# Attention with relative bias and a squared-ReLU feed-forward layer: products of 128 rows split into two row tiles of TensorE, the lower half behind the upper

## The chip, the cores and the metric

The kernel runs on one core of one Trainium2 chip. The metric is the device time of one execution in microseconds. PE is TensorE, DVE VectorE, ACT ScalarE, POOL GpSimd, SP SyncE; SP computes nothing here, its queue issues DMAs.

## The reference

Eight batches of eight heads, 576 positions, head size 64; then a feed-forward layer over the 4608 rows of 512.

```python
scores = 1.0 / np.sqrt(D) * np.matmul(q, k.transpose(0, 1, 3, 2))
scores = scores + bias_table[bucket].transpose(2, 0, 1)[None]     # bucket depends on |i - j| alone
scores = scores - np.max(scores, axis=-1, keepdims=True)
attn = np.exp(scores)
attn = attn / (np.sum(attn, axis=-1, keepdims=True) + 1e-09)
x = np.matmul(attn, v).transpose(0, 2, 1, 3).reshape(B * S, H * D)
h = np.maximum(x @ w_in, 0.0)                                     # 512 -> 2048
out = h * h @ w_out                                               # 2048 -> 512
```

Inputs and output are float32; the kernel works in float16 with float32 sums.

## The kernel before

**Attention.** A pair is two heads of one batch (32 pairs). Their q and k are turned so that head 0 lies on partitions 0 to 63 and head 1 on 64 to 127: on PE for the first two batches (L947), by DMA_TRANSPOSE issued on SP from the third on (L930). Scores come transposed, keys on partitions: for each block of 128 keys one matmul per head with 64 contracted rows and up to 512 queries (L815), one head on the upper 64 rows of PE's array, one on the lower 64, side by side. The last 64 queries go in eight matmuls of 64 columns (L822); the last 64 keys of both heads share one block, `kz`, that has zeros elsewhere, and use all 128 rows (L1012, L879). ACT takes exponentials out of PSUM into `pt` and `pm`, and DVE multiplies the diagonal bands by the bias's exponentials. The product with V (`values`) contracts 128 keys: for each tile of 128 queries one matmul of 130 columns with `pm` (L754) and eight of 65 with `pt` (L761); the 65th column gives the sum for the division. DVE divides into `x`, which is turned into `xt` by PE (L1078, first two batches) or by DMA_TRANSPOSE on SP (L795).

**Feed-forward.** Nine groups of 512 rows. The first layer has plain units of 128 x 512 (L1501, L1451) and units of seven products instead of eight (`by_sevens`, L1378). The second layer (`second`, L1204) also has seven products instead of eight, as 14 atoms of eight matmuls of 256 columns, all 128 rows. DVE and ACT read the sums out; SP issues the stores (L1260) and the loads of V from the third batch on (L368), POOL casts V.

**Order.** Nothing is issued as the loops run. Each step is an `Op` with costs by engine, dependences and buffers; `Plan.schedule` lays all of them out engine by engine, the earliest possible first and, among those, the least due time. `DUES` is a long table of due times that replaces those of some operations. The program is written in the order of the planned starts, and each engine works through its own part in that order. PE's mode in the plan is "r" for scores (64 rows) and "f" for the rest; a change of mode is charged with `SWITCH`. PSUM has two pairs of banks for scores (`sets_ps`, ring `r_set`) and four single banks (`g_ps`, ring `r_g`).

Of the kernel before, what the change touches and what calls it, by code (L numbers as in the profile page):

```python
# [30 lines left out]
DT_QK = 2  # L31
PERIOD, LEAD, FAST, FASTN = 8500, 2000.0, 3300.0, 6
# [93 lines left out]
class Ring:  # L126


    def __init__(self, n, in_order=False):
        self.free = [(0.0, i) for i in range(n)]  # L130
        self.in_order, self.made, self.taken = in_order, 0, 0


class Buf:


    def __init__(self, ring):
        self.ring, self.left, self.slot, self.until = ring, 0, None, 0.0
        self.turn, ring.made = ring.made, ring.made + 1


class Op:
    __slots__ = (
        "engs", "fn", "deps", "bufs", "due", "after", "mode",
        "users", "wait", "ready", "eng", "start", "end", "seq", "spare", "packets",
    )

    def __init__(self, engs, fn, deps, bufs, due, after, mode):
        self.engs, self.fn, self.bufs, self.due = engs, fn, bufs, due
        self.after, self.mode = after, mode  # L150
        self.deps = [d for d in deps if d is not None]
        self.users, self.ready, self.spare = [], after, 0.0
        self.start = self.end = self.eng = None
# [6 lines left out]
AGAIN = {"ACT": 30.0, "DVE": 30.0}  # L160

# [9 lines left out]
STAY = 0.0  # L171


class Plan:
# [3 lines left out]
    def add(self, engs, fn, deps=(), bufs=(), due=0.0, after=0.0, mode=None):  # L178
        op = Op(engs, fn, deps, list(bufs), due, after, mode)
        op.seq = len(self.ops)  # L180
        self.ops.append(op)
        for b in op.bufs:
            b.left += 1
        return op
# [6 lines left out]
    def schedule(self):  # L191
# [4 lines left out]
        for op in self.ops:  # L196
            op.wait = len(op.deps)
            for d in op.deps:
                d.users.append(op)
            if not op.wait:  # L200
                for e in op.engs:
                    waiting[e].append(op)
# [67 lines left out]
def act(n):  # L270
    return 174.0 + n / 1.2
# [1337 lines left out]
```

## Time and profile before

| | before |
|---|---|
| device time, two runs | 358.85 and 359.93 us, median 359.39 |
| profiled execution | span 358.7 us from first to last instruction, 0.7 us under the median |
| PE matmuls | x4290 |
| granted TensorE clock | 1.000 |
| PE, DVE, ACT, POOL busy | 97%, 83%, 76%, 48% |
| DMA | 44.37 MB, mean 124 GB/s |

The span is that of one execution; a run's time also holds what lies around it. A matmul's row lasts from its start until its results are out, so rows of neighbouring matmuls overlap, and PE counts as busy for as long as any of them runs.

### The profile page before, as it was taken

The numbers are of one execution on the slowest core, as the hardware profiler recorded it, in microseconds if no ns is written. First come the engines' busy times: TensorE is split into PE (matmuls) and PEld (weight loads), VectorE is DVE, ScalarE is ACT, GpSimd is POOL, SyncE is SP. The second block draws the span as 40 slices with busy tenths as digits, with TensorE's granted clock in tenths as the row PEclk, the third lists the DMA queues.
The fourth block names the chain that finished last, engine by engine and source line by source line (L and its number), as shares of the span: only waits on it lengthen the run. The fifth ranks groups of instructions, "written<-read, shape, count | busy, mean of one in ns | idle before, by whom it ended". The sixth has DMA issues, their size and how long they took to land.

```text
span 358.7 us, 10742 instructions
## 1 busy us (share of the span) xinstructions
PE 346.4 (97%) x4290; PEld 262.0 (73%) x4290; DVE 297.5 (83%) x673; ACT 272.6 (76%) x435; POOL 170.6 (48%) x289
## 2 busy tenths in 40 slices
PE   3988999999999999999999999999999999999996
PEld 3666788775587558877788568755867887888885
DVE  4888999666996799768896899798988798899993
ACT  4898997589966988678976887689889833899830
POOL 8886679698995896158478456221000000000000
PEclk9999999999999999999999999999999999999999
DMA  9999999999999999799999999863410032010023
GB/s 172 151 147 198 193 150 154 190 156 192 175 130 165 223 158 112 119 163 198 84 134 164 186 126 133 150 121 72 61 44 15 18 97 68 27 63 33 23 66 117
DMA packets 162210, 44.37 MB, mean 124 GB/s; under 512 B 145520, under 2 KB 162160, under 8 KB 162160
## 3 DMA queue, kind: packets, MB, share of 16 engines
q0 software_dynamic: 74208, 14.53, 54.6%
q1 hardware_dynamic: 87696, 28.86, 44.3%
q8 instruction: 33, 0.54, 0.6%
q10 hardware_dynamic: 256, 0.30, 0.3%
q14 instruction: 17, 0.14, 0.1%
HBM read 36.94 MB, written 9.44 MB: 129 GB/s over the span
## 4 chain that ended last, share of the span: by engine, by line
PE 88%; DMA 7%; POOL 2%; ACT 1%; issue 1%; DVE 0%; POOLq 0%
PE f L1204 31%; PE f L1501 20%; PE f L761 10%; PE st L815 8%; PE f L1378 7%; DMA w_in_sb<-in_moe_w_in_dram 5%; PE f L1451 3%; PE st L1378 3%; PE f L754 3%; PE st L1012 2%; DMA ks<-in_k_dram 2%; POOL va L368 2%; PE f L822 1%; PE f L1078 1%; POOL ks L368 0%
## 5 line engine op out<-in xcount | busy, mean ns | idle before, releaser
L997 ACT ACTIVATE pt<-st 128x1024 f16<-128x1024 f32 x112 | 111.1, 1031 | 23.0 <-PE st L815 22.8
L1501 PE MATMUL f<-xt,w_in_sb 128*128 128x512 f16 (+4 forms) x416 | 77.2, 330 | 0.0
L728 DVE TENSOR_TENSOR pt<-pt,tb_sb 128x512 f16<-128x512 f16 (+3 forms) x108 | 61.9, 581 | 12.6 <-ACT pt L997 9.3
L368 POOL DMA_DIRECT2D ks<-in_k_dram x79 | 55.9, 719 | 15.1 <-DMA kt<-ks 10.4
L1204 PEld LDWEIGHTS <-g 128*128 128x128 f16 x576 | 55.1, 98 | 7.6 <-issue 0.8
L368 POOL DMA_DIRECT2D qs<-in_q_dram x79 | 55.5, 712 | 8.1 <-DMA qt<-qs 6.2
L1530 ACT ACTIVATE rt<-f 128x512 f16<-128x512 f32 x80 | 47.3, 608 | 14.1 <-PE f L1501 12.7
L1501 PEld LDWEIGHTS <-w_in_sb 128*128 128x128 f16 x416 | 37.1, 98 | 26.7 <-issue 2.5
L761 PE MATMUL f<-va,pt 128*128 128x65 f16 x1280 | 53.2, 193 | 0.3 <-DMA va<-in_v_dram 0.3
L761 PEld LDWEIGHTS <-pt 128*128 128x128 f16 x1280 | 49.8, 97 | 1.3 <-issue 0.5
L1204 PEld LDWEIGHTS <-s 128*128 128x128 f16 x432 | 41.1, 98 | 5.8 <-issue 0.8
L1232 DVE SCALAR_TENSOR_TENSOR y<-f,y 128x512 f32<-128x512 f32 (+1 forms) x48 | 31.8, 665 | 12.5 <-PE f L1204 11.7
L815 PE MATMUL st<-qt,kt 64*128 64x512 f16 (+1 forms) x288 | 40.4, 361 | 1.0 <-DVE qt L716 0.6
L1540 DVE TENSOR_TENSOR g<-rt 128x512 f16<-128x512 f16 x80 | 34.3, 433 | 6.2 <-ACT rt L1530 5.3
L1204 PE MATMUL f<-wt,g 128*128 128x256 f16 x288 | 35.6, 273 | 0.0
L754 PE MATMUL f<-vm,pm 128*128 128x130 f16 x160 | 35.5, 222 | 0.0
L1204 PE MATMUL f<-w_out_sb,s 128*128 128x256 f16 x288 | 35.3, 273 | 0.0
L1204 PE MATMUL f<-w_out_sb,g 128*128 128x256 f16 x288 | 34.7, 273 | 0.1
L780 DVE TENSOR_TENSOR x<-f,r 128x384 f16<-128x384 f32 (+1 forms) x64 | 30.9, 485 | 0.9
L645 POOL CAST va<-f 128x512 f16<-128x512 f32 x24 | 16.7, 702 | 30.8 <-DMA f<-in_v_dram 17.5
L974 POOL COPY kz<-kt 64x64 f16<-64x64 f16 x55 | 19.4, 354 | 20.2 <-DMA kt<-ks 17.1
L831 ACT ACTIVATE pt<-f 128x256 f16<-128x256 f32 x64 | 22.9, 404 | 5.9 <-PE f L822 4.5
(112 smaller groups left out, 532.4 us busy)
## 6 DMA issues: line engine op xcount, KB each, us to landing
out_dram<-y SPq DMA_DIRECT2D x34, 256.0 KB, 2.8
f<-in_v_dram SPq DMA_DIRECT2D x24, 256.0 KB, 4.9
ks<-in_k_dram POOLq DMA_DIRECT2D x48, 64.0 KB, 5.2
qs<-in_q_dram POOLq DMA_DIRECT2D x48, 64.0 KB, 4.4
w_in_sb<-in_moe_w_in_dram POOLq DMA_DIRECT2D x4, 512.0 KB, 10.7
w_out_sb<-in_moe_w_out_dram POOLq DMA_DIRECT2D x4, 512.0 KB, 8.9
ks<-in_k_dram POOLq DMA_DIRECT2D x7, 144.0 KB, 5.6
qs<-in_q_dram POOLq DMA_DIRECT2D x7, 144.0 KB, 5.5
```

The source lines that it names most:

```text
L368: lambda: io(eng.dma_start(out=out_(), in_=in_())),
L728: io(nc.vector.tensor_tensor(out=a, in0=a, in1=t, op=MULT))
L754: nc.tensor.matmul(ps[:, i, :, :], pm[:, c : c + 128], vm[:, hp, :, 0:65], start=True, stop=False)
L761: nc.tensor.matmul(ps[:, i, e, :], pt[:, (2 * jt + e) * S + c : (2 * jt + e) * S + c + 128], va[:, jt, 2 * hp + e, 0:65], start=False, sto ...
L815: nc.tensor.matmul(banks[i][:, e, :], kt[rw[e], ts(jt, 128)], qt[rw[e], ds(q0, n)], start=True, stop=True)
L997: nc.scalar.activation(out=p5(pts[pb.slot])[:, jt, :, 0:512], in_=sets_ps[st.slot], func=EXPF, scale=SCALE)
L1204: nc.tensor.matmul(home[bf.slot][:, ts(s_, HALF)], left(c, s_), right(c), start=(c == 0 and (s_ == 0 or apart) and (own or i not in before ...
L1232: nc.vector.scalar_tensor_tensor(out=dst, in0=ps, scalar=OSC, in1=ys[y[plus].slot][:, cs], op0=MULT, op1=mybir.AluOpType.add,)
L1378: nc.tensor.matmul(ps()[:, ds(HALF * f + a, z - a)], left()[:, kk, ts(f, 128)], right(a, z)[:, kk, :], start=(first_ and f == 0 and a == 0 ...
L1501: nc.tensor.matmul(g_ps[bank.slot][:, a:z], w_in_sb[:, kk, ts(nt, 128)], xt_sb[:, kk, c : c + z - a], start=(kk == 0), stop=(kk == 3),)
L1530: io(nc.scalar.activation(out=rts[rb.slot], in_=g_ps[bank.slot], func=RELUF))
L1540: nc.vector.tensor_tensor(out=gs[gb1.slot][:, nt, :], in0=rts[rb.slot], in1=rts[rb.slot], op=MULT)
```

## The change

Between planned times of 48 and 291 us (`LAG_ON`, `LAG_OFF`), every product of 128 rows is written as two of 64 rows: the upper half on the upper row tile, then, later, the lower half on the lower row tile, into the same bank of PSUM, where it adds to the upper half's sums. On PE's queue the halves of two neighbouring operations are interleaved by their planned starts. Scores go on as before, one head on each tile, without a change of mode around them. Since the two halves of one product write one bank, the lower may only start when the upper has ended; the function `after` puts a nop on SP between them that waits for the last upper matmul and that the first lower one waits for. Before 48 and after 291 us the products keep all 128 rows. PSUM becomes one ring of eight banks; scores take two neighbouring ones. The last queries of both heads share a pair of banks and one exponential (two before). From the third batch on (`APART`), scores are asked for one block of keys at a time. `DUES` has an entry for nearly each operation, with other values.

The constants, the split and the nop:

```diff
+PV = 28.5
+APART = 2
+LAG_ON, LAG_OFF, MARGIN = 48000.0, 291000.0, 260.0
+SINGLES, PAIRS = 2, 8
 DUES = """
-0:1620 2:1057 4:1180 10:1374 14:10158 16:8662 20:10687 22:11516 35:2669 52:4535 56:9455 58:7112 60:7916 68:10815
...
+0:2103 2:737 4:910 6:8661 8:21837 10:893 11:10541 12:15763 13:7333 14:7972 15:6893 16:10135 17:18456 18:10786
...
+    rows_of = {None: slice(0, 128), 0: slice(0, 64), 1: slice(64, 128)}
+    def matmuls(made):
+        def parts(tile_):
+            rw = rows_of[tile_]
+            def one(out_, lhsT, rhs, first):
+                return lambda: io(
+                    nc.tensor.matmul(
+                        out_, lhsT[rw], rhs[rw], start=first and tile_ != 1, stop=True, skip_group_check=True
+                    )
+                )
+            return [(ns, one(out_, lhsT, rhs, first)) for ns, out_, lhsT, rhs, first in made()]
+        return parts
...
+    def after(earlier):
+        between = io(nc.sync.nop())
+        sync = mybir.DependencyInfo(mybir.DependencyClass.Sync, mybir.DependencyReason.DATA)
+        tc.add_manual_dep(between.ins, earlier.ins.name, sync, reason="row tiles")
+        return lambda ins: tc.add_manual_dep(ins.ins, between.ins.name, sync, reason="row tiles")
+
+    emit(P.schedule(), after)
```

The product with V, where a half of the `pm` matmul needs the columns of its own head alone:

```diff
             for i in range(nq):
                 c = (qt0 + i) * 128
-                io(
-                    nc.tensor.matmul(
-                        ps[:, i, :, :], pm[:, c : c + 128], vm[:, hp, :, 0:65], start=True, stop=False
-                    )
-                )
+                es = slice(0, 2) if tile_ is None else slice(tile_, tile_ + 1)
+                one(ps[:, i, es, :], pm[rw, c : c + 128], vm[rw, hp, es, 0:65], i == 0 and tile_ != 1)
                 for e in range(2):
                     for jt in range(4):
...
+                        one(
+                            ps[:, i, e, :], pt[rw, (2 * jt + e) * S + c : (2 * jt + e) * S + c + 128],
+                            va[rw, jt, 2 * hp + e, 0:65],
                         )
...
-        o = P.add({"PE": nq * 300.0}, pv, deps + l_v[b, hp] + first, [bank, pb, b_v[b]], T + 1, after, "f")
+        o = on_pe(nq * 300.0, nq * 9 * PV, PV, pv, deps + l_v[b, hp] + first, [bank, pb, b_v[b]], T + 1, after)
```

In the plan, an operation of kind 2 (a split product) starts its lower half at `t1`, behind the lower tile's earlier work and at least `MARGIN` behind its upper half; kind 1 (scores) takes both tiles, its lower head put between the lower products:

```diff
+        if op.kind == 2:
+            t1 = max(st.now1, at + took + MARGIN)
+            st.now1 = op.t1 = t1
+            st.now1 += took
+            st.behind.append([op, t1, t1 + took])
+            return at, t1 + took
+        t1 = at
+        if st.behind and st.behind[0][1] < at:
+            x, qs, qe = st.behind[0]
+            t1 = min(qe, qs + np.ceil((at - qs) / x.lmm) * x.lmm)
+            op.within, op.rest = x, qe - t1
```

What this makes of PE's queue, at two places in the middle of the program. First, a product with V before: `pm`'s block of 130 columns is the first of a query tile, `pt`'s of 65 columns follow; a weight load stands ahead of each matmul.

```order
L754 LDWEIGHTS pm
L754 MATMUL f_121<-vm,pm 128x130
L761 LDWEIGHTS pt
L761 MATMUL f_121<-va,pt 128x65
L761 LDWEIGHTS pt
L761 MATMUL f_121<-va,pt 128x65
```

And after, where the lower half of a product with V (L1170) ends, next to the second layer (L764, `s_98` and `g_101` are its left operands); the bracket names the semaphores that an instruction waits for.

```order
L764 LDWEIGHTS s_98
L764 MATMUL bank<-wt,s_98 128x256
L1170 LDWEIGHTS pt
L1170 MATMUL bank<-va,pt 128x65
L764 LDWEIGHTS g_101 [waits SP_sequencer_49]
L764 MATMUL bank<-w_out_sb,g_101 128x256
L764 LDWEIGHTS s_98
L764 MATMUL bank<-wt,s_98 128x256
L764 LDWEIGHTS g_101
L764 MATMUL bank<-w_out_sb,g_101 128x256
```

The product with V has turned into halves with 65 columns throughout. `s_98` rows are upper halves of one atom, `g_101` rows lower halves of the atom before it; the first of these waits for SP, and every row behind it stands behind that wait.

Second, a little further on: scores of one pair (L777, keys `kt_83`) with the lower half of the atom `s_98`.

```order
L764 LDWEIGHTS s_98 [waits SP_sequencer_49]
L764 MATMUL bank<-wt,s_98 128x256
L777 LDWEIGHTS kt_83
L777 MATMUL bank<-qt_79,kt_83 128x512
L777 LDWEIGHTS kt_83
L777 MATMUL bank<-qt_79,kt_83 128x512 [waits DVE_49]
L764 LDWEIGHTS s_98
L764 MATMUL bank<-wt,s_98 128x256
```

The first L777 matmul is head 0 on the upper tile, the second head 1 on the lower one. Six more lower `s_98` matmuls follow before the upper tile's next matmul, one of 64 columns; before the change the two scores stood next to each other with full products on both sides.

On SP, five transposing DMAs in a row before (`x` to `xt` L795, q and k L930):

```order
L795 DMA_TRANSPOSE xt_95<-x1_92 128x3x128 [waits DVE_49]
L795 DMA_TRANSPOSE xt_95<-x0_91 128x3x128 [waits DVE_49]
L930 DMA_TRANSPOSE qt3_81<-qs2_72 128x5x128 [waits DMASW4_49,DMASW3_49,DMAHW1_49,DMASW2_49,PE_49]
L795 DMA_TRANSPOSE xt_95<-x1_92 128x2x128 [waits DMAHW2_49]
L930 DMA_TRANSPOSE kt3_85<-ks2_73 128x5x128 [waits DMASW7_49,DMAHW3_49,DMASW6_49,DMASW5_49]
```

And five after (L1212 and L1341 are the same lines):

```order
L1341 DMA_TRANSPOSE kt1_83<-ks1_71 128x5x128 [waits PE_49,DMASW7_49,DMAHW7_49,DMASW5_49,DMASW3_49]
L1212 DMA_TRANSPOSE xt_95<-x2_93 128x2x128 [waits PE_49,DMAHW0_49]
L1212 DMA_TRANSPOSE xt_95<-x3_94 128x2x128 [waits PE_49,DMAHW1_49,DVE_49]
L1341 DMA_TRANSPOSE qt3_81<-qs2_72 128x5x128 [waits PE_49,DMASW7_49,DMASW6_49,DMAHW2_49,DMASW5_49]
L1212 DMA_TRANSPOSE xt_95<-x0_91 128x3x128 [waits PE_49,DMAHW3_49,DVE_49]
```

The nops have no rows of their own here; what they wait for stands in the bracket of the next row. Nearly every DMA on SP now has one or more waits for PE ahead of it. The program has 329 of these nops; on PE 316 waits for SP stand, some of which cover two nops. PE's program has 6903 matmuls instead of 4289.

More of the change, by code (lines that the diff above doesn't have):

```diff
@@ L176, in __init__, with add @@
         self.ops = []
[L178 to L179 removed]
+    def add(self, engs, fn, deps=(), bufs=(), due=0.0, after=0.0, mode=None, kind=0, ltook=0.0, lmm=1.0, order=()):
+        op = Op(engs, fn, deps, list(bufs), due, after, mode, kind, ltook, lmm, order)
         op.seq = len(self.ops)
@@ L189, in land, with _over_for, _start_on_pe @@
         return op
+    @staticmethod
+    def _over_for(u, d):
+        if tuple(u.engs) == (d.eng,):
+            return d.end + (MARGIN if d.lag else AGAIN.get(d.eng, 0.0))
+        return d.end + LAT[d.eng]
+    def _start_on_pe(self, op, at):
+        st = self
+        if st.lagging and at >= LAG_OFF:
+            at = max(at, st.now1)
+            st.lagging, st.behind, st.mode = False, [], "lag"
+        if not st.lagging and op.kind and LAG_ON <= at < LAG_OFF:
+            if st.mode != "lag":
+                at += SWITCH
+            st.lagging, st.now1, st.behind, st.mode = True, at, [], "lag"
+        if st.lagging and not op.kind:
+            at = max(at, st.now1) + SWITCH
+            end = op.t0end = at + op.engs["PE"]
+            st.now["PE"] = st.now1 = end + SWITCH
+            st.behind = []
+            return at, end
+        if not st.lagging:
+            took = op.engs["PE"]
+            if op.mode != st.mode:
+                took += SWITCH
+                st.mode = op.mode
+            st.now["PE"] = op.t0end = at + took
+            return at, at + took
+        op.lag, took = True, op.ltook
+        st.now["PE"] = op.t0end = at + took
+        st.behind = [x for x in st.behind if x[2] > at]
+        if op.kind == 2:
[9 more added lines that the diff above has]
+            op.within, op.rest = x, qe - t1
+        op.t1, end = t1, t1 + took
+        prev = end
+        for x in st.behind:
+            if x[2] <= t1:
+                continue
+            if x[1] < t1:
+                by = took
+            else:
+                by = prev - x[1]
+                if by <= 0:
+                    prev = x[2]
+                    continue
+                x[1] += by
+                x[0].t1 = x[1]
+            x[2] += by
+            prev = x[0].end = x[2]
+            for b in x[0].bufs:
+                until = x[2] + LAT["PE"]
+                if until > b.until:
+                    b.until = until
+                    if not b.left:
+                        b.ring.free = [
+                            (until, i) if last is b else (t, i) for t, i, last in (f + (b.ring.last[f[1]],) for f in b.ring.free)
+                        ]
+            for u in x[0].users:
+                if not u.wait and u.start is None:
+                    u.ready = max(u.ready, self._over_for(u, x[0]))
+        if st.behind:
+            st.now1 = max(st.now1, st.behind[-1][2])
+        st.now1 = max(st.now1, end)
+        return at, end
@@ L202, in schedule @@
                     waiting[e].append(op)
+            for b in op.bufs:
+                b.ring.last = {}
         done = []
@@ L223, in schedule @@
             (at, _, _), e, op = best
-            took = op.engs[e]
-            if e == "PE" and op.mode != mode:
-                took += SWITCH
-                mode = op.mode
             for x in op.engs:
                 waiting[x].remove(op)
-            op.eng, op.start, op.end = e, at, at + took
-            now[e] = op.end - (over(e, took, op))
+            op.eng = e
+            if e == "PE":
+                op.start, op.end = self._start_on_pe(op, at)
+            else:
+                took = op.engs[e]
+                op.start, op.end = at, at + took
+                op.t0end = op.end
+                now[e] = op.end - over(e, took, op)
             for b in op.bufs:
                 if b.slot is None:
-                    t, b.slot = min(b.ring.free)
-                    b.ring.free.remove((t, b.slot))
+                    b.slot = self._take(b, op.start)
                     b.ring.taken += 1
+                    b.before = [b.ring.last[i] for i in range(b.slot, b.slot + b.size) if i in b.ring.last]
                 b.left -= 1
@@ L239, in schedule @@
                 if not b.left:
-                    b.ring.free.append((b.until, b.slot))
-            for u in op.users:
+                    for i in range(b.slot, b.slot + b.size):
+                        b.ring.free.append((b.until, i))
+                        b.ring.last[i] = b
+            for u in op.users + op.followers:
                 u.wait -= 1
                 if not u.wait:
-                    u.ready = max(
-                        [u.after]
-                        + [d.end + (LAT[d.eng] if tuple(u.engs) != (d.eng,) else AGAIN.get(d.eng, 0.0)) for d in u.deps]
-                    )
+                    u.ready = max([u.after] + [self._over_for(u, d) for d in u.deps] + [d.t0end for d in u.order])
                     for x in u.engs:
@@ new lines, in _buf_time @@
+    def _buf_time(self, op, at):
+        taken, left = {}, None
+        for b in op.bufs:
+            if b.slot is not None:
+                continue
+            if b.ring.banks:
+                left = list(b.ring.free) if left is None else left
+                got = self._pick(left, b)
+                if got is None:
+                    return None
+                at = max(at, got[0])
+                left = [x for x in left if not got[1] <= x[1] < got[1] + b.size]
+                continue
+            i = taken[b.ring] = taken.get(b.ring, -1) + 1
+            if len(b.ring.free) <= i or (b.ring.in_order and b.turn != b.ring.taken + i):
+                return None
+            at = max(at, sorted(b.ring.free)[i][0])
+        return at
@@ new lines, in _take @@
+    def _take(self, b, start):
+        free = b.ring.free
+        if not b.ring.banks:
+            got = min(free)
+        elif b.size == 2:
+            got = self._pick(free, b)
+        else:
+            at = {i: t for t, i in free}
+            got = None
+            for t, i in sorted((x for x in free if x[1] >= SINGLES), key=lambda x: x[1]):
+                score = 0
+                if t <= start:
+                    score = 2 if at.get(i ^ 1, 1e18) > start else 1
+                if got is None or score > got[2] or (score == got[2] and (score or t < got[0])):
+                    got = (t, i, score)
+        b.ring.free = [x for x in free if not got[1] <= x[1] < got[1] + b.size]
+        return got[1]
@@ L374, in loader, with by_heads, parts, one @@
         return P.land(packets, [issue], list(bufs) + lane, spare[0]), issue
+    rows_of = {None: slice(0, 128), 0: slice(0, 64), 1: slice(64, 128)}
[7 more added lines that the diff above has]
+                    )
+                )
+            return [(ns, one(out_, lhsT, rhs, first)) for ns, out_, lhsT, rhs, first in made()]
+        return parts
+    def by_heads(made):
+        def parts(tile_):
+            def one(out_, lhsT, rhs):
+                return lambda: io(nc.tensor.matmul(out_, lhsT, rhs, start=True, stop=True))
+            pairs = [[(ns, one(*x)) for x in both] for ns, both in made()]
+            return [x for both in pairs for x in both] if tile_ is None else [both[tile_] for both in pairs]
+        return parts
+    def on_pe(ns, lns, lmm, parts, deps, bufs, due, after=0.0, mode="f", order=(), kind=2):
+        return P.add({"PE": ns}, parts, deps, bufs, due, after, mode, kind, lns, lmm, order)
     def one_of(engs, fn, deps, bufs, due):
```

379 lines of the change are left out of this document (231 added, 148 removed), and 267 rows, old and new, of the table DUES.

## The prediction

> **What bounds the kernel now.** I read the page's busy shares and its chain first, then the span in three stages, then PE's own timeline.
>
> ```profile
> span 358.7 us, 10742 instructions
> ...
> PE 346.4 (97%) x4290; PEld 262.0 (73%) x4290; DVE 297.5 (83%) x673; ACT 272.6 (76%) x435; POOL 170.6 (48%) x289
> ...
> PE 88%; DMA 7%; POOL 2%; ACT 1%; issue 1%; DVE 0%; POOLq 0%
> ```
>
> ```profile
> 0.00:48.00 48.00, 38.91 (x706) 30.02 (x706) 38.14 (x111) 39.62 (x64) 36.30 (x67) 1.00 1.35 171
> 48.00:291.00 243.00, 242.90 (x2981) 175.78 (x2980) 202.17 (x460) 194.57 (x304) 134.28 (x222) 1.00 1.16 132
> 291.00:360.00 69.00, 64.55 (x607) 56.24 (x605) 57.15 (x105) 38.42 (x67) 0.00 (x0) 0.99 0.18 58
> ```
>
> The third number of a stage is PE's busy time. Between 48 and 291 us PE is busy for 242.90 of 243.00 us: nothing that ACT, DVE or a queue does reaches the end of this kernel there, and whatever holds PE back adds to the time in full. PE waits only in the first 48 us (9.1 us) and after its last matmul, whose row below (353.64 + 1.91, less 0.16 as shown next) puts its end at 355.4: 3.3 us. "Busy" can still hide poor use, so I look at how closely matmuls follow each other.
>
> ```profile
> 113.08 1.36 PE L1204 MATMUL f<-w_out_sb,s 128*128 128x256 f16 x11
> 114.37 0.60 PE L815 MATMUL st<-qt,kt 64*128 64x512 f16 x4
> 114.82 0.28 PE L822 MATMUL f<-qt,kt 64*128 64x64 f16 x8
> 115.03 0.50 PE L1204 MATMUL f<-wt,g 128*128 128x256 f16 x3
> 343.16 3.66 PE L1204 MATMUL f<-w_out_sb,g 128*128 128x256 f16 x32
> 353.64 1.91 PE L1204 MATMUL f<-wt,g 128*128 128x256 f16 x16
> 101.56 0.22 PE L754 MATMUL f<-vm,pm 128*128 128x130 f16 x1
> 101.62 0.41 PE L761 MATMUL f<-va,pt 128*128 128x65 f16 x8
> 101.86 0.22 PE L754 MATMUL f<-vm,pm 128*128 128x130 f16 x1
> ```
>
> ```profile
> L1204 PE MATMUL f<-w_out_sb,g 128*128 128x256 f16 x288 | 34.7, 273 | 0.1
> L822 PE MATMUL f<-qt,kt 64*128 64x64 f16 x256 | 9.0, 190 | 0.0
> L761 PE MATMUL f<-va,pt 128*128 128x65 f16 x1280 | 53.2, 193 | 0.3 <-DMA va<-in_v_dram 0.3
> PEld L815 <- issue: 12.8, 48, 0.4
> ```
>
> In a merged row the last matmul's own length comes off: 32 of 256 columns take (3.66 - 0.27) / 31 = 0.109 us each. Eight of 64 columns run as four pairs, one on each row tile: (0.28 - 0.19) / 3 = 0.03 us a pair. One query tile of the product with V takes 101.86 - 101.56 = 0.30 us: 0.06 for the 130 columns, eight times 0.03 for the others. These lie on 0.417 ns a column plus 2.5 ns, in either mode. A matmul's row is longer than its spacing by 0.16 us (273 against 109 ns, 190 against 29): results come out that much later. A change of tile shape costs about 0.1 us: the last L1204 row ends its streaming at 113.08 + 11 x 0.109 = 114.28, the scores start at 114.37; the weight load is what waits (the row "issue", 48 times).
>
> **What the change removes.** Counted in the built order, neighbours on PE with unlike tile shapes fall from 154 to 45: 109 x 0.096 = 10.5 us. Of the 160 query tiles, 140 trade their 130 columns (57 ns) for 65 on each tile at once (30 ns): 3.8 us. Twenty of the 40 x transposes pay 64 columns for 128: 0.5 us. Everything else is split evenly: 256 columns over 64 rows, twice, side by side, cost the same 0.109 us. Summed by shape, PE's columns and switches come to 344.0 us before and 329.2 after (235.2 on the upper tile, as many on the lower, 81.6 full, 8.2 turning q and k, 4.3 in switches): **-14.8 us**. Bounds: no gain, if a split pair cannot keep the pace of the 64-row pairs above, to -14.8.
>
> **What it adds inside PE's queue.** Upper and lower halves stand in one queue. A matmul starts when the one ahead has started and its own tile is free; laying each order on its tiles with the spacings above, without any wait, gives 344.2 us for before (the trace's PE ends 355.4 after 11.2 us of waits, so this is sound) and 344.1 for after: 13.6 us of empty upper tile eat the gain. One such place is shown in the order: behind a score matmul of 0.22 us on the upper tile stand a lower one and seven lower products, 0.98 us, before the upper tile gets its next matmul. The gaps come from halves of unlike length next to each other. Bounds: 0, if the tiles slide freely past each other, to +14.9; I take **+14.8**, since the queue is one.
>
> [...]
>
> **What it adds on SP.** A lower half may not start before its upper half is done. The kernel makes this sure with a nop on SP: PE now waits 316 times for SP (284 times at a lower half's first weight load, 32 times at an upper half that needs an earlier lower one), and SP each time for PE: a handshake. SP's queue also issues every transposing DMA, each V load and each store, in order.
>
> ```profile
> L795 SPq DMA_TRANSPOSE xt<-x x48: 1168/1206/2377, 89.7 to 298.6; - x48
> L930 SPq DMA_TRANSPOSE qt<-qs x24: 1198/1230/2972, 53.4 to 249.4; - x24
> L930 SPq DMA_TRANSPOSE kt<-ks x24: 1198/1224/2892, 55.4 to 250.8; - x24
> L795 SPq EVENT_SEMAPHORE  x30: 17/17/12251, 89.6 to 298.6; - x30
> L368 SPq DMA_DIRECT2D f<-in_v_dram x36: 372/532/781, 52.2 to 232.2; - x36
> ```
>
> ```profile
> 119.91 1.29 SPq L930 DMA_TRANSPOSE qt<-qs  x1
> 121.37 2.56 SPq L930 DMA_TRANSPOSE kt<-ks  x2
> 124.05 1.20 SPq L930 DMA_TRANSPOSE qt<-qs  x1
> 125.36 1.18 SPq L1260 DMA_DIRECT2D out_dram<-y  x1
> 133.27 0.28 PE L822 MATMUL f<-qt,kt 64*128 64x64 f16 x8
> 133.59 1.23 SPq L930 DMA_TRANSPOSE qt<-qs  x1
> 6.09 0.15 ACT L424 ACTIVATE ex_sb<-f 128x8 f16<-128x8 f32 x1
> 6.24 0.42 PEld L947 LDWEIGHTS <-ks 96*64 96x64 f16 x10 [1.36 <-ACT ex_sb L424]
> ```
>
> The columns are least, median and greatest length in ns. A free SP answers quickly: 0.16 us until results are out, 0.04 from PE's end (133.55) to SP's start (133.59), 0.02 to 0.03 for the semaphore instruction, next to nothing back to the weight load (6.24 to 6.24): 0.25 us with rounding. In the order the waiting half mostly stands 0.22 to 0.87 us behind the end that it waits for; 50 of the 316 stand closer than 0.25, 2.8 us in all, of which running tiles cover some: **+2 us** (0 to 2.8).
>
> A busy SP does not answer. Four transposes in a row start 1.3 us apart, and each holds the queue for its 1.2 us. In the order, 94 handshakes have a transpose between them and the handshake ahead. For the 81 with one transpose alone, PE's distance from one upper end to the next is 0.92 us on average and the lower half has 0.14 us to spare beyond the 0.25: 1.27 - 0.92 - 0.14 = 0.21 us late, 19.1 us over those that are late at all. Ten have a copy too: 1.82 - 0.96 - 0.14 = 0.72, 7.3 us. The rest adds 1.9: 28.3 us, if each DMA is issued at once when the handshake ahead is through. With the least lengths (1.17) it is 22 us; with 1.4 a piece, as long rows up to 2.97 suggest, 45. A lateness also moves the next transpose, and a DMA that waits for DVE's x or y holds the handshake behind it just as long (the semaphore row: up to 12.25 us of SP waiting on x): carrying each delay on to the next raises 28 to about 40, and letting no DMA go before its place in the order to 54. I take **+36**, between the first sum and the carried one. Nothing hides it: behind the waiting lower weight load stand the upper tile's next matmuls, and PE is the bound. What DVE, ACT and POOL gain in slack is worth nothing.
>
> **The rest.** One pool of eight banks and one exponential for both heads' last queries change ACT and PSUM, which PE does not wait for: 0, between -2 and +2. The new due times reorder the first 48 us; of 9.1 us idle there the 4.41 until the first DMA stays, so -4.7 to +5; I take 0. PE now reads 13,805 weight loads and matmuls instead of 8,577; the trace shows no PE wait for instructions that I could scale; 0 to +5, taken 0.
>
> **Sum** on the profiled execution: 358.7 - 14.8 + 14.8 + 2 + 36 = 396.7. The span lies 0.7 below the median of the two runs (359.39), so **397 us**. Its own range is 380 (22 us of SP) to 415 (54).
>
> **Rivals.** *The tiles run free and SP keeps up* (the other side): every nop meets an idle SP, as where no DMA lies between handshakes (182 of 316), and the tiles fill each other's gaps: 359.4 - 14.8 = 345. It decides if a transpose holds SP for less than about 1.0 us of another instruction's time; against it stand the 1.2 us rows, with never another SP row inside. *SP keeps up, the queue's gaps stay*: 359.4 + 2 = 361, no change; for it, that gaps where PE waits anyway also give SP time. *Ends in order*: if a short matmul on one tile cannot end before a longer one ahead of it on the other, unlike neighbours run at the longer one's pace; laid out so, the order takes 384.5 us instead of 344.1, and with SP's transposes 411; with 14.5 us of waits at start and end and 0.7 outside the span, 426. In the trace every pair on two tiles has equal lengths (L815, L822), which decides nothing. [...]
>
> **Chances.** Forecast 0.64; ends in order 0.12; no change 0.14; free tiles 0.10. Two per cent, 7 us, is about what two measurements of this kernel can tell from no change: faster below 352, slower above 367. So faster 0.10, same 0.14, slower 0.76. The range 357 to 424 leaves out the free tiles (0.10), part of the ordered ends (0.06) and the bottom of no change (0.03).
>
> **What would show it.** Right: PE's weight loads wait hundreds of times for SP, some 0.3 to 0.6 us each, behind DMA_TRANSPOSE rows; PE's share of the span falls below 92% between 48 and 291 us; DVE's and ACT's busy time stays, spread over more. The removed switches show as few or no "issue" waits of L777. Wrong: SP's event rows answer within 0.25 us although transposes surround them, or PE's busy share stays at 97% with a shorter span. If 64-row halves of 256 columns follow each other by more than 0.109 us without any wait, the order of ends is the cause, not SP.

## The result

| | before | after |
|---|---|---|
| device time, median of two runs | 359.39 us (358.85 to 359.93) | 422.0 us (421.25 to 422.75) |
| ratio, 95% interval | | 1.173, 1.164 to 1.182 |
| profiled span | 358.7 us | 419.4 us |

The change makes the kernel 17% slower: 62.6 us. The prediction had the side and the main cause. The time lies 25 us above its point, above the 380 to 415 of the forecast itself, and just inside the stated range of 357 to 424, whose upper end was there for a rival.

The profile of after, first its page: the span, the busy shares, the chain of work that ended last, and the queue that brings instructions.

```profile
span 419.4 us, 16276 instructions
...
PE 366.7 (87%) x6904; PEld 296.0 (71%) x6904; DVE 303.2 (72%) x681; ACT 274.0 (65%) x398; POOL 166.7 (40%) x287
...
q8 instruction: 54, 0.88, 0.9%
...
PE 59%; SPq 14%; issue 7%; DVE 7%; DMA 5%; ACT 4%; POOL 3%; POOLq 0%; ACTq 0%
```

PE alone carried 88% of the chain before; now it has 59%, and SP's queue, which was not in it, 14%. DVE's and ACT's work has hardly grown (297.5 and 272.6 us before); its shares fell because the span grew.

The first two of the three stages, for after (span of the stage, busy time of PE, its weight loads, DVE, ACT and POOL; the last three columns are the granted clock of PE, the share of the DMA engines and GB/s):

```profile
0.00:48.00 48.00, 38.49 (x695) 29.74 (x696) 35.60 (x107) 39.73 (x61) 36.07 (x66) 0.96 1.37 171
48.00:291.00 243.00, 208.99 (x4294) 163.38 (x4294) 164.74 (x364) 156.92 (x217) 129.24 (x217) 0.99 1.04 121
```

The first 48 us are nearly as before (38.91 us of PE then; the granted clock was 0.96 in them, against 1.00). Between 48 and 291 PE stands quite still for 34 us, where it was 0.1. What it waits for, from the view of waits (engine, line, releaser: us in all, times, longest):

```profile
PEld L764 <- SPq L1994: 48.9, 79, 2.1
PEld L1170 <- SPq L1994: 14.7, 19, 2.1
PEld L777 <- issue: 3.7, 11, 0.7
PE bank L764 <- SPq L1994: 27.0, 54, 1.8
PE bank L1170 <- SPq L1994: 9.4, 13, 1.8
```

L1994 is the nop on SP. Weight loads wait 64 us for it in some hundred places, 0.65 us a time; in 36 us of that nothing runs on PE at all, in the rest the row of some matmul still runs. The waits of the scores (L777, L815 before) for a new tile shape fell from 48 to 11, as counted.

One of these waits in full, SP's and PE's weight loads' timelines (start, length, engine, line; the bracket is the idle time ahead and what ended it):

```profile
195.38 1.93 SPq L1341 DMA_TRANSPOSE kt<-ks  x1
195.94 0.15 PEld L764 LDWEIGHTS <-sw 64*128 64x128 f16 x4
197.41 0.09 PEld L764 LDWEIGHTS <-w_in_sb 64*128 64x128 f16 x1 [1.32 <-SPq L1994]
197.42 0.09 PEld L764 LDWEIGHTS <-sw 64*128 64x128 f16 x1
```

The transposing DMA ends at 197.31, SP runs the nop, and 0.1 us later the lower half's weight load starts; behind it, 0.01 us on, stands the upper tile's next weight load, which had waited for nothing but its turn.

### The profile page after: what moved, and what is told of

It is laid out like the page before. It is cut to its first block, busy times and chain, and to the rows that moved or that the text cites. A ratio compares the mean times of both kernels' runs of the same rounds, so it can differ in the third digit from the quotient of the medians.

```text
span 419.4 us, 16276 instructions
## 1 busy us (share of the span) xinstructions
PE 366.7 (87%) x6904; PEld 296.0 (71%) x6904; DVE 303.2 (72%) x681; ACT 274.0 (65%) x398; POOL 166.7 (40%) x287
## 4 chain that ended last, share of the span: by engine, by line
PE 59%; SPq 14%; issue 7%; DVE 7%; DMA 5%; ACT 4%; POOL 3%; POOLq 0%; ACTq 0%
PE bank L764 44%; PE bank L1170 9%; SPq L1341 7%; PE bank L777 5%; SPq L1212 4%; ACT pt L1412 2%; DMA va<-in_v_dram 2%; DVE pt L1140 2%; SPq L747 1%; DVE g L1957 1%; DMA ks<-in_k_dram 1%; DMA kt<-ks 1%; DMA g<-in_k_dram 1%; POOL va L747 1%; ACT rt L1947 1%
## 5 line engine op out<-in xcount | busy, mean ns | idle before, releaser
L764 PE MATMUL bank<-xt,w_in_sb 64*128 64x512 f16 (+7 forms) x1144 | 156.8, 309 | 8.6 <-SPq L1994 7.8
L1412 ACT ACTIVATE pt<-bank 128x1024 f16<-128x1024 f32 x112 | 112.4, 1030 | 41.2 <-PE bank L777 37.2
L764 PEld LDWEIGHTS <-w_in_sb 64*128 64x128 f16 (+1 forms) x1260 | 91.7, 95 | 30.4 <-SPq L1994 18.0
L764 PEld LDWEIGHTS <-g 64*128 64x128 f16 (+1 forms) x976 | 83.7, 95 | 22.7 <-SPq L1994 14.6
L1170 PE MATMUL bank<-va,pt 64*128 64x65 f16 (+1 forms) x2400 | 93.6, 190 | 2.9 <-DMA va<-in_v_dram 1.6
L1170 PEld LDWEIGHTS <-pt 64*128 64x128 f16 (+1 forms) x2400 | 82.0, 94 | 5.2 <-issue 2.7
L764 PEld LDWEIGHTS <-s 64*128 64x128 f16 (+1 forms) x720 | 62.6, 95 | 21.9 <-SPq L1994 15.3
L764 PE MATMUL bank<-w_out_sb,s 64*128 64x256 f16 (+1 forms) x480 | 64.8, 273 | 9.4 <-SPq L1994 9.2
L764 PE MATMUL bank<-w_out_sb,g 64*128 64x256 f16 (+1 forms) x504 | 68.1, 270 | 4.9 <-SPq L1994 4.7
L1140 DVE TENSOR_TENSOR pt<-pt,tb_sb 128x512 f16<-128x512 f16 (+3 forms) x108 | 61.1, 575 | 14.6 <-ACT pt L1412 10.0
L777 PE MATMUL bank<-qt,kt 64*128 64x64 f16 (+2 forms) x544 | 69.7, 280 | 0.5 <-ACT pt L1279 0.5
L764 PE MATMUL bank<-wt,g 64*128 64x256 f16 (+1 forms) x472 | 64.0, 274 | 3.2 <-SPq L1994 3.2
L1170 PE MATMUL bank<-vm,pm 64*128 64x65 f16 (+1 forms) x300 | 55.3, 194 | 10.0 <-SPq L1994 9.4
L747 POOL DMA_DIRECT2D qs<-in_q_dram x79 | 55.8, 713 | 19.9 <-DMA qt<-qs 16.1
L1170 PEld LDWEIGHTS <-pm 64*128 64x128 f16 (+1 forms) x300 | 27.4, 94 | 16.2 <-SPq L1994 14.7
L777 PEld LDWEIGHTS <-kt 64*128 64x128 f16 x544 | 30.6, 95 | 7.2 <-issue 3.7
L1192 DVE RECIPROCAL r<-bank 128x6 f32<-128x6 f32 (+1 forms) x64 | 11.8, 186 | 30.8 <-PE bank L1170 30.4
```

Source lines behind the costliest of these rows:

```text
L747: lambda: io(eng.dma_start(out=out_(), in_=in_())),
L764: nc.tensor.matmul(out_, lhsT[rw], rhs[rw], start=first and tile_ != 1, stop=True, skip_group_check=True)
L777: return lambda: io(nc.tensor.matmul(out_, lhsT, rhs, start=True, stop=True))
L1140: io(nc.vector.tensor_tensor(out=a, in0=a, in1=t, op=MULT))
L1170: nc.tensor.matmul(out_, lhsT, rhs, start=first, stop=True, skip_group_check=True)
L1412: nc.scalar.activation(out=p5(pts[pb.slot])[:, jt, :, 0:512], in_=sets_ps[st.slot], func=EXPF, scale=SCALE)
```

## The experiments

Eight kernels were run. Beside them, before took 359.4 to 360.0 us. Where no spread is given, the kernel ran once.

**The split with PE's own wait.** The nop is put on PE, just ahead of the lower half; it turns into a wait of the weight load for PE's own semaphore. SP has no part. The order and all else stay.

```diff
+        if ns is not None and op.lag:
+            for x, o in needs(e, op):
+                known[x, id(o)]()
         ins = fn()
...
-        between = io(nc.sync.nop())
...
+            between = io(nc.tensor.nop())
```

> Same split, same order, but PE waits for its own semaphore at the lower half's first weight load; no nop on SP, so no handshake. Theory A (SP's queue answers late because transposing DMAs stand in it, some 64 us of PE's waits after the change): at least 55 us go, 422 becomes 345 to 365. Within A: if the row tiles slide past each other, as starts out of queue order in the trace after the change suggest, 345 to 352; if the gaps of the queue order stay, as the prediction had it, 358 to 365. Theory B (the wait for the upper half itself is long, or short matmuls end behind longer ones on the other tile): above 395.

Measured: 372.15 us (370.88 to 373.01), 1.033 of before (1.029 to 1.038). Its page, its middle stage and the longest of its waits behind 48 us:

```profile
PE 349.6 (95%) x6904; PEld 301.9 (82%) x6904; DVE 301.8 (82%) x681; ACT 270.9 (73%) x398; POOL 171.5 (46%) x287
...
48.00:291.00 243.00, 235.44 (x5291) 205.54 (x5290) 199.79 (x448) 186.28 (x265) 135.51 (x222) 1.00 1.19 131
...
PEld L1171 <- issue: 7.8, 11, 1.8
PEld L765 <- issue: 5.0, 11, 2.0
PEld L765 <- PE bank L765: 1.1, 5, 0.3
```

The way over SP costs 50 us (422.0 - 372.15): that is shown, since order, banks and work are the same. PE's wait for itself costs next to nothing: 1.1 us in five places (the last row). That a lower half has to wait for its upper half is taken from the kernel; no run goes without the wait. But 372 is neither the 361 of "SP keeps up, the queue's gaps stay" nor the 345 of "free tiles": some 12 us are lost without SP.

**The same handshakes, with plain DMAs.** The 96 transposing DMAs become plain copies in SBUF, so q, k and x are not turned; the nops stay on SP (the same line at both places, for x and for q and k).

```diff
-                        nc.sync.dma_start_transpose(
+                        nc.sync.dma_start(
```

> The nops stay on SP, but the 96 transposing DMAs of q, k and x are replaced by plain copies of the same tiles, which SP issues in about 0.5 us instead of 1.2 (the output is not the reference's: q, k and x are not turned). Theory A: 96 times 0.7 us less in SP's queue, at most 67 us; most of it stood in PE's way, so 365 to 385. Theory B: nothing changes on PE, 415 to 425.

Measured: 377.07 us. A DMA now holds SP for 0.465 us, and PE's waits for SP shrink from 64 to 15 us:

```profile
L1341 SPq DMA_DIRECT2D kt<-ks x24: 464/465/1216, 58.2 to 263.0; - x24
...
PEld L764 <- SPq L1994: 12.2, 35, 1.4
PEld L1170 <- SPq L1994: 2.2, 5, 0.7
```

So 45 of the 50 us go when the transposing DMAs do, 5 belong to the rest of SP's queue. The transfers themselves are other ones too; what ties the 45 us to their time on the queue is that PE's waits for SP shrink by about as much.

**The nop on ACT.**

```diff
-        between = io(nc.sync.nop())
+        between = io(nc.scalar.nop())
```

> The nop stands in ACT's queue instead of SP's. ACT is busy 65% of the time with instructions of 0.6 to 1.0 us that PE's own results feed. Theory A (any busy queue between the halves holds PE): as slow as on SP or slower, 410 to 460. If only SP's DMA issues are to blame in some way of their own: 350 to 370.

Measured: 375.45 us. I had expected ACT, with activations of 1.03 us, to hold the nops as SP does; it does not:

```profile
PEld L764 <- ACTq L1994: 3.0, 13, 0.4
PEld L1170 <- ACTq L1994: 1.0, 4, 0.3
```

No wait for ACT lasts more than 0.4 us. A busy engine is thus not the point: a nop passes while an activation runs. The nop's own rows (EVENT_SEMAPHORE of L1994, 17 ns each) show it; here two of them, which end at 64.87 and 65.37, stand inside one activation of 1.04 us:

```profile
64.37 1.04 ACT L1412 ACTIVATE pt<-bank 128x1024 f16<-128x1024 f32 x1
L1994 ACTq EVENT_SEMAPHORE  x2: 17/17/17, 64.8 to 65.4; - x2
```

Of the 329 nops on ACT 176 stand well inside an activation's row. Of the 329 on SP in after none stands inside the row of a DMA, and 110 come 45 to 60 ns after the end of one. Which part of ACT lets a nop pass was not tried.

**The change without the split.** The window in which products are split is empty; due times, banks, exponentials and single blocks of scores stay.

```diff
-LAG_ON, LAG_OFF, MARGIN = 48000.0, 291000.0, 260.0
+LAG_ON, LAG_OFF, MARGIN = 1e9, 1e9, 260.0
```

> The changed kernel without split products: one ring of PSUM banks, one exponential for the last queries, scores by single blocks, the new due times. Theory A (the loss is the handshake's alone): 358 to 368, as before the change, since the switches of tile shape are back. If the rest of the change costs something by itself: 370 to 385.

Measured: 374.38 us, 14 to 15 us over before. Counted in the built order, changes of tile shape are 231 here, against 154 before (77 more at some 0.1 us each, about half of the difference; the other half was not traced), and the weight loads that wait for them show it:

```profile
PEld L777 <- issue: 19.6, 66, 0.9
PEld L764 <- issue: 18.0, 61, 1.0
PEld L1170 <- issue: 5.4, 20, 0.7
```

The table of due times belongs to the split; without it the same table gives another order. So this run does not price "the rest" of the change by itself, and the next one keeps the order instead.

**The same order, products whole.** Each split product is written with all 128 rows at the place of its upper half; operations and banks stand in the order of after.

```diff
-        elif not op.lag:
+        elif True:
```

> The changed kernel's own order of operations, bank by bank the same, but each product written whole, with 128 rows, where its upper half stood; no lower halves, no handshakes. With nothing split a change of tile shape stands at both sides of every group of scores: 248 in the built order, 23.7 us, and laid out without waits it takes 353.0 us (329.3 for the split order if tiles slide freely, 344.1 in a strict queue). Theory that the split gives back on the queue nearly all that it saves: 353 + 12.4 us at the start and behind the last matmul + 0.7 outside the span + 0 to 8 us of waits = 366 to 374, within 5 us of the 372 of the split with PE's own wait. Rival, that the halves side by side bring their whole saving: 24 us above 372, so 390 to 396.

Measured: 379.6 us (378.55 to 380.33), 1.056 of before (1.054 to 1.059), some 6 us above the 366 to 374 that I expected and well under the rival's 390. In one order the split, with PE's own wait, is worth 7.5 us (372.15 against 379.6), not the 24 us of its columns and switches alone, nor nothing.

**Shorter exponentials.** On the split with PE's own wait, the exponentials of full score blocks cover 256 of 512 columns.

```diff
-                            out=p5(pts[pb.slot])[:, jt, :, 0:512], in_=sets_ps[st.slot], func=EXPF, scale=SCALE
+                            out=p5(pts[pb.slot])[:, jt, :, 0:256], in_=sets_ps[st.slot][:, :, 0:256], func=EXPF, scale=SCALE
```

> Split with PE's own wait (372 us), but the exponentials of full score blocks cover 256 of 512 columns: 0.43 us less each on ACT, so score banks come free and DVE's work starts sooner; PE's program is the same. In the trace of the 372 us run about 10 us of empty row tile behind 48 us stand behind a matmul that waits for ACT, DVE or a DMA, and 18 us behind one that only waits for its own tile. Theory that most of the loss is frozen in the order of the queue: only the 10 us can go, 360 to 366. Rival, that PE waits for banks at run time and nothing else holds it: 350 to 355. Rival, that ACT has no part: 370 to 373.

Measured: 370.36 us (369.07 to 371.74), 1.030 of before (1.026 to 1.034), with 41 us less of ACT:

```profile
PE 349.7 (95%) x6904; PEld 300.9 (82%) x6904; DVE 301.3 (82%) x681; ACT 229.9 (63%) x398; POOL 172.9 (47%) x287
```

1.8 us at best: in this order of PE's queue, banks or exponentials that come late at run time are not what holds PE. The theory that I put first (10 us) is refuted; the 10 us had come from a rough match of rows to the order, which a better one (below) puts at 3.6.

**Two row tiles by themselves.** Streams of 64-row matmuls, each pattern on its own line: blocks of m on the upper tile, then m on the lower (L62 to L68: m = 1, 2, 3, 4, 6, 8, 16), one of 512 columns against seven of 64 (L69), four of 256 against fourteen of 65 (L70), 64 pairs of 65 (L73); then twelve products of 8 x 256 columns, the lower half three rows behind the upper: banks apart (L103), one bank with PE's own wait (L104), with a nop on an idle SP (L105), with a transposing DMA ahead of each nop (L106).

```python
def blocks(m, n, total):
    return [(e, n) for _ in range(total // m) for e in range(2) for _ in range(m)]
```

> Nothing of the reference is computed: TensorE alone, streams of 64-row matmuls on the two row tiles, each pattern on a line of its own, 6 full matmuls between patterns. Blocks of m matmuls of 256 columns on the upper, then m on the lower tile, 32 (33, 36) on each. Strict queue (a matmul starts only once the one ahead has started): 3.5, 3.7, 5.0, 5.4, 6.7, 6.3, 6.7 us for m = 1, 2, 3, 4, 6, 8, 16. Tiles that slide freely: 3.5, 3.5, 3.6, 3.5, 3.9, 3.5, 3.5. Sliding by at most four rows: 3.5, 3.5, 3.6, 3.5, 4.2, 3.9, 5.7. Eight times four of 256 columns above and fourteen of 65 below: 5.8 strict, 4.4 with four rows, 3.5 free. Eight times one of 512 above and seven of 64 below: 1.7, but 3.1 if ends too must follow the order. [...] Then twelve products of 8 x 256, the lower half three rows behind the upper: 11.5 us in banks of their own; in one bank with PE's own wait 11.5 to 12; with a nop on an idle SP 11.5 to 13 (0.25 us for an answer, 0.33 to spare); with one transposing DMA ahead of each nop 16 to 18 (1.25 us and more for each of twelve).

Groups of its matmuls (the first number behind the bar is PE's busy time in us, which has 0.16 us behind the last start's columns in it; the number behind the second bar is idle time):

```profile
L106 PE MATMUL bank<-x,w 64*128 64x256 f16 x187 | 13.2, 270 | 4.1 <-SPq L95 4.1
L105 PE MATMUL bank<-x,w 64*128 64x256 f16 x187 | 11.2, 269 | 0.0
L104 PE MATMUL bank<-x,w 64*128 64x256 f16 x187 | 11.2, 269 | 0.0
L103 PE MATMUL bank<-x,w 64*128 64x256 f16 x187 | 10.9, 269 | 0.0
...
L68 PE MATMUL bank<-x,w 64*128 64x256 f16 x64 | 5.9, 270 | 0.0
L66 PE MATMUL bank<-x,w 64*128 64x256 f16 x72 | 4.3, 269 | 0.0
L67 PE MATMUL bank<-x,w 64*128 64x256 f16 x64 | 4.2, 270 | 0.0
...
L65 PE MATMUL bank<-x,w 64*128 64x256 f16 x64 | 3.7, 269 | 0.0
...
L70 PE MATMUL bank<-x,w 64*128 64x256 f16 x32 | 3.7, 269 | 0.0
...
L73 PE MATMUL bank<-x,w 64*128 64x65 f16 x128 | 2.1, 190 | 0.0
...
L69 PE MATMUL bank<-x,w 64*128 64x512 f16 x8 | 1.9, 377 | 0.0
L69 PE MATMUL bank<-x,w 64*128 64x64 f16 x56 | 1.8, 190 | 0.0
```

Less 0.16: 3.5 to 3.6 us up to blocks of four, 4.1 for six, 4.1 for eight, 5.7 for sixteen; four of 256 against fourteen of 65 in 3.5; one of 512 against seven of 64 in 1.7. For blocks of four, six, eight and sixteen and for L70 a strict queue would need 5.4, 6.7, 6.3, 6.7 and 5.8, and for L69 a queue whose ends follow its order 3.1. An estimate from these five rows, and no more than a fit: laid out with the spacings above so that a row may start ahead of up to three that stand before it and wait for the other tile, they come to 3.49, 4.15, 3.93, 5.68 and 3.49, all within 0.15 us. What PE does inside is not shown. Unlike lengths next to each other cost nothing in L69 and L70, which take the 1.7 and 3.5 us of their longer tile's columns alone; runs of six rows and more for one tile do cost (at 0.109 us a row, 32 rows on each tile take 3.5 us and the 36 of the blocks of six 3.9). And a handshake over an idle SP costs as little as PE's own wait, (11.2 - 10.9) / 12 = 0.03 us; with a transposing DMA ahead of each it costs (13.2 + 4.1 - 11.2) / 12 = 0.51 us: lower halves mostly start 1.32 us apart there, at the pace of the DMAs on SP, against 0.93 us of matmuls, and one DMA of 2.3 us adds 1.1 us more.

**The supply of instructions.** 960 pairs of 65 columns in turn on the two tiles (L75), 320 pairs of 256 (L76), and both again while SP issues 30 loads of 256 KB (L77, L78).

> Nothing of the reference is computed: TensorE alone, matmuls of 64 rows in turn on the two row tiles, four stretches, 6 full matmuls behind each: 960 pairs of 65 columns, 320 pairs of 256 columns, and both again while SP issues 30 loads of 256 KB in 256-byte packets. The trace of the split with PE's own wait has six places, the same in the run with the nops on ScalarE, where PE waits 0.2 to 2.0 us for nothing that the profile shows, 7.6 us in all; each ends 1.2 to 1.5 us after a 16 KB packet of the instruction queue has landed, that is 256 instructions or 64 pairs here. Theory that PE runs out of instructions where they go by faster than blocks are fetched: 64 pairs of 65 columns take 1.9 us, a packet of 0.9 to 1.3 us and 1.4 us behind it 2.3 to 2.7, so each of some 15 blocks adds 0.4 to 0.8 us: 35 to 41 us instead of 28.4 for the first stretch, 41 to 50 for the third (packets of up to 1.9 us beside other transfers); 64 pairs of 256 columns take 7.0 us, so 35 us for the second and fourth. Rival, that blocks are fetched well ahead and the six waits are something else: 28.4, 35, 28.4 to 29 and 35.

Its groups, and a piece of PE's timeline in the first stretch:

```profile
L77 PE MATMUL bank<-x,w 64*128 64x65 f16 x1920 | 38.0, 204 | 19.5 <-issue 19.5
L76 PE MATMUL bank<-x,w 64*128 64x256 f16 x640 | 35.1, 269 | 0.0
L78 PE MATMUL bank<-x,w 64*128 64x256 f16 x640 | 35.1, 269 | 0.0
L75 PE MATMUL bank<-x,w 64*128 64x65 f16 x1920 | 33.9, 194 | 20.4 <-issue 20.4
```

```profile
21.93 2.12 PE L75 MATMUL bank<-x,w 64*128 64x65 f16 x128 [1.10 <-issue]
25.38 2.12 PE L75 MATMUL bank<-x,w 64*128 64x65 f16 x128 [1.33 <-issue]
28.84 2.12 PE L75 MATMUL bank<-x,w 64*128 64x65 f16 x128 [1.33 <-issue]
...
47.48 2.12 PE L75 MATMUL bank<-x,w 64*128 64x65 f16 x128 [1.88 <-issue]
51.21 2.12 PE L75 MATMUL bank<-x,w 64*128 64x65 f16 x128 [1.61 <-issue]
```

PE runs 128 matmuls, that is 256 instructions with their weight loads, stands for 1.3 to 1.9 us, and so on: at first 3.46 us for each 256 instructions, later 3.73 and 4.00, 3.77 on average. The stretch takes 54.3 us instead of 28.4, with no transfer under way but the instructions' own. The granted clock was 1.00 up to 52 us, so the steps and their growth are not the clock's. Pairs of 256 columns are not touched (64 pairs take 7.0 us). The expectation had the cause and a quarter to a half of its size. With the loads the stretch takes 57.5 us; the granted clock was 0.77 in 30 us of it, so the 3 us more are not the loads' alone.

## Why the prediction came out as it did

**What bounds the kernel: right.** PE's stillness between 48 and 291 us went from 0.1 to 34 us and the time followed; 41 us less of ACT moved it by 1.8.

**The saving of 14.8 us in columns and switches: right as a count.** Spacing is as assumed: L73 runs 64 pairs of 65 columns, 128 matmuls, in 1.95 us, 0.030 a pair. Of the parts, the table below shows the switches' alone (11.8 to 1.5 us, where 10.5 were forecast).

**The gaps in PE's queue, +14.8: near in size, wrong in rule.** To see where the row tiles stand empty I matched each matmul's row in the trace to its place in the built order, tile by tile, and asked for each moment at which a tile is empty what the first unstarted row of the queue waits for; times are those of both tiles halved, behind 48 us. The match is a reconstruction, so its rows are good to about 2 us.

| us | before | PE's own wait | after |
|---|---|---|---|
| only that its own tile is taken | 0.2 | 12.5 | 11.9 |
| the handshake (SP, or PE itself) | - | 2.1 | 57.8 |
| nothing: no wait, and its own tile free | 0.1 | 9.6 | 4.9 |
| ACT, DVE, POOL or a DMA | 0.2 | 3.6 | 1.6 |
| changes of tile shape, spacing | 11.8 | 1.5 | 2.2 |
| all | 12.3 | 29.3 | 78.4 |

Two steps of the prediction's sentence fail. The queue is not one strict line: by the match, some 700 of the 6903 matmuls of after start ahead of a row that stands before them, and laid out as the five rows of the two-tile run suggest (the estimate above) the same order, without any wait, takes 337.3 us, not 344.1. And "halves of unlike length next to each other" is not the reason, by L69 and L70. Of the 14.6 us in the first two rows of the table (PE's own wait), 8.0 are in the order itself (337.3 - 329.3), and 4.6 come up when PE's own waits, taken as 0.25 us behind each end, are laid in (341.9); both figures are estimates from that layout, not measured. That the sum still came near the 14.8 is in part luck: a strict queue that isn't there stood for waits that the prediction had counted elsewhere. In the plan's own start times (a plan, not a measurement) the upper tile stands empty for 16.1 us between 48 and 291 us, 12.3 of them in 37 places where no bank of PSUM is free for the next product, since a split product keeps its bank through both halves. That the order's gaps come from there was not tried on the chip.

**SP, +2 and +36: right in cause, too small by a quarter to a third; the mis-sized term of the sum.** Taking SP out brought 50 us, of which 45 go with the transposing DMAs; in the table the waits of after are 57.8. The prediction took off, at nearly each of 94 handshakes, 0.14 us that the lower half had to spare, and 0.92 us between ends, from 1.27. But where transposing DMAs follow one another, the spare is used up once: in the two-tile run they cost 0.51 us each, and by an estimate from that 94 x 0.51 = 48. And the DMAs held SP for longer than the median that the prediction went by:

```profile
L1212 SPq DMA_TRANSPOSE xt<-x x48: 1167/1182/1865, 97.0 to 359.4; - x48
L1341 SPq DMA_TRANSPOSE kt<-ks x24: 1199/1208/2104, 59.6 to 299.5; - x24
L1341 SPq DMA_TRANSPOSE qt<-qs x24: 1199/1209/2454, 62.4 to 303.5; - x24
```

The 96 rows have a median of 1.20 us, but 25 of them exceed 1.3, and the mean is 1.32. In before, 25 exceeded 1.3 too, with a mean of 1.41: this stood in the trace that the prediction was made from. The forecast "hundreds of waits of 0.3 to 0.6 us" was some hundred of 0.65.

**The rest, taken as 0: wrong by some 5 us in after, by 10 without SP's waits, in the instructions.** The bound of 0 to +5 for the instruction fetch was named, and its lower end taken. Of the 9.6 us "nothing" above (PE's own wait), 7.6 fall at six places of PE's program; in the trace of the run with PE's own wait, PE's timeline at the first of them:

```profile
65.97 0.28 PE L1171 MATMUL bank<-va,pt 64*128 64x65 f16 x4
67.88 0.27 PE L765 MATMUL bank<-wt,s 64*128 64x256 f16 x1 [1.64 <-issue]
67.89 0.20 PE L1171 MATMUL bank<-va,pt 64*128 64x65 f16 x1
```

They lie at matmuls 1117, 1245, 2012, 3671, 3798 and 4563 of the queue, at nearly the same place in a block of 128 matmuls each time, and the run with the nop on ACT has stops at 1117, 1245, 2012, 3671 and 3798 too (and at 2267). Each ends 1.2 to 1.6 us behind the end of a 16 KB packet on the instruction queue. One such packet goes with 256 instructions: the page of the run with PE's own wait has 54 of them, 0.88 MB, for 6904 matmuls and as many weight loads, and the 3840 instructions of L75 came with 15. Two lower and two upper instructions in 30 ns, as in the product with V, ask for 256 instructions in 1.9 us, faster than the 3.46 to 4.00 us measured above; pairs of 256 columns, with 7.0 us for 256 instructions, did not stand (L76). That PE lacks instructions at these places is what the packets and the stops after 128 matmuls suggest; the runs show no more than that. New due times and single blocks of scores stay unpriced: no run changes them in an order that stays the same.

**The sum.** From before to PE's own wait, spans: +10.4 us (358.7 to 369.1). From the table: -14.8 + 12.3 + 2.1 + 9.5 + 3.4 = +12.5. From there to after: +50.3 (369.1 to 419.4), and from the table 78.4 - 29.3 = 49.1. From before to after directly: +60.7, and from the last column -14.8 + 11.7 + 57.8 + 4.8 + 1.4 = +60.9, where the prediction had -14.8 + 14.8 + 38 + 0. Of the 25 us by which it fell short, some 20 are thus the handshake, 5 the instructions, 1 other waits and 2 lie outside the span, less 3 of gaps that it had too large. The time lies inside the stated range only because the range was drawn up to 424 for the ordered ends, a mechanism that is refuted; by the forecast's own reasoning it would have ended at 415. That part is luck.

**The rivals.** "Ends in order" (426) lay nearest to the result, but its mechanism is refuted: with SP out of the way the time is 372, L69's seven of 64 columns run beside one of 512 in 1.7 us (3.1 if ends kept the order), and L70's fourteen of 65 beside four of 256 without loss. "Free tiles and an SP that keeps up" (345) and "the queue's gaps stay" (361) both assumed that SP answers; on an idle SP it does, in 0.03 us, but the transposing DMAs are there. Even without SP the split does not win here: the best form of it that does the whole work, with PE's own wait, is 3.3% slower than before, and none of these kernels beats the kernel before.

## What to carry to other kernels

A wait between two of TensorE's own instructions belongs on TensorE: by way of a queue that issues DMAs it costs whatever issue stands there, here 0.51 us for each transposing DMA (L106), for the whole array, where PE's own wait cost 0.03 (L104). Splitting a product into row tiles pays only as far as the queue feeds both tiles in turn, here in runs of up to four (3.5 us; runs of sixteen took 5.7), and, if the plan's own start times are right, as far as there are banks for products that are held for longer. Before many small matmuls replace few large ones, set the time that 256 instructions take on TensorE against the 3.46 to 4.00 us of L75.

## What the hardware showed beyond that

- With 32 matmuls of 64 rows and 256 columns on each row tile, blocks of four in turn ran at full pace (3.5 us), blocks of sixteen took 5.7.
- In a long run (L75) PE got 256 instructions in 3.46 to 4.00 us; with 65 columns on both tiles it stands 38% of the time (20.4 of 54.3 us).
- A nop on ACT passes while an activation runs (176 of 329), and PE waits for it 0.4 us at most, with ACT busy for 73% of the span; on SP a transposing DMA being issued holds it to the end, 1.2 to 2.5 us.
